# A two-stage bf16 kernel on one core: the order of a tie convolution, its copies and V's second half in the second and third bundle

## The chip, the core and the metric

The kernel runs on one core of one Trainium2 chip. The time is the device time of one execution in microseconds (us). A profile of one execution is at hand: what each engine did and when. The engines are TensorE (PE: matmuls, and PEld: weight loads), VectorE (DVE), ScalarE (ACT), GpSimd (POOL, which here issues loads) and SyncE (SP, which issues stores and transposing reads).

## The reference

First a causal convolution of 7 taps along the sequence, with one softmax-normalised set of taps for each of 8 heads of 24 columns. Its result goes into a channel mix: two mixtures of each row with the row before it, a projection to 1024 with relu and square, a projection back to 192, and a sigmoid gate.

```python
# x: 8 x 4160 x 192, weight: 8 x 7
out = einsum('hk,bskhg->bshg', softmax(weight), windows_of_7(x))     # -> x of the next part
x_prev = shift_by_one_row(x)
xk = mu_k * x + (1.0 - mu_k) * x_prev
xr = mu_r * x + (1.0 - mu_r) * x_prev
k = np.maximum(xk @ w_k, 0.0)          # 192 -> 1024
v = k * k @ w_v                        # 1024 -> 192
r = 1.0 / (1.0 + np.exp(-(xr @ w_r)))
return (r * v).astype(np.float32)
```

## The kernel before

The batch is worked in four pairs of sequences. A pair's 4160 rows are cut into steps of 512 rows (the first step of the first pair has 256). A step has eight **slots** (four for the step of 256). A slot is: the K matmuls of 128 of the 1024 hidden columns for both sequences into one PSUM tile of two banks (`k_mm`, L465, matmul L481), a relu out of PSUM on ScalarE (`k_relu`, L493), and a square on VectorE (`k_square`, L507). Four slots in a row make a **bundle**. So bundle 0 is step 0, bundles 1 and 2 are step 1, and so on. The text calls bundle 1 the second and bundle 2 the third; slot 2.1 is the first slot of the second bundle.

A **quad** is 256 rows of both sequences: the gate's matmuls and its sigmoid (`r`, L538 and L546), the V matmuls back to 192 columns (`v_rows`, L566, in two halves), the product with the gate (`v_out`, L582) and two stores (L590). The first quad is worked in the third bundle.

The convolution is a product with a banded matrix, over blocks of 120 rows. The rows are loaded by groups of blocks (`x_tile`, L100, with its memsets L106, L108 and L110; `load_x`, L112, with DMAs L120, L125 and L126 on GpSimd's queue); three buffers hold groups. The first three groups of the first pair (the **tie**) are convolved straight into the transposed layout that the mix needs: `conv_t` (L319), and `to_yT` (L329) copies the 128 x 480 fp32 result from PSUM to bf16. The second bundle does this for group 2, in three parts of 64 columns. Later groups go through `conv_mm` (L299) in units of two PSUM banks, and `conv_out` (L345), a ScalarE copy to a tile y. Group 3 is then transposed by TensorE (`tr`, L390, copies L399); from group 4 on, y goes to DRAM (`y_write`, L368) and comes back transposed (`y_read`, L376).

A unit of `conv_mm`, and a quad's V, is worked in two halves. In each half the upper and the lower 64 rows of the array write different banks; in the second half they change places. Between the halves stands an empty ScalarE instruction (`clobber_nop`, L307 and L574, called the **ticket** here): it waits for the first half, and the second half waits for it. It stands in ScalarE's order like any other instruction.

PSUM is one ring of four tiles of two banks (tag "k"), shared by slots, tie tiles, convolution units, gate, V and transposes. A tile that is asked for takes the buffer that is free next, and its first matmul waits until the last reader of that buffer is done.

The order is written by hand (`manual_schedule`): each engine runs its instructions in the order in which the functions `bundle_first`, `bundle_second` and `bundle_rest` call them. Work that has a due bundle stands in tables (`early`, `mix_a`, `mix_b`, `mix_c`, `late`, `rq`, `xt`, `vq`; L618), filled at L629 to L683 with `at`, and `run(table, b)` puts that bundle's entries at that point. `early` runs ahead of the bundle. In the second bundle `mix_a` runs after slot 2.4's matmuls and slot 2.1's square (L784, L785).

In `bundle_second` the three tie copies go to ScalarE, VectorE and ScalarE. In `bundle_rest` the third bundle (b == 2) has branches of its own: it transposes group 3 (L818 to L822), and its order after slot 3.3 is at L825 to L829 and L835 to L841.

Of the kernel before, what the change touches and what calls it, by code (L numbers as in the profile page):

```python
# [14 lines left out]
def kernel(  # L15
# [44 lines left out]
    for p in range(NPAIR):  # L60
# [5 lines left out]
        for L in sizes:  # L66
            ns = L * NF // STEP
# [210 lines left out]
    def conv_units(g):  # L278

        if groups[g][2] * 4 * G <= BANK:  # L280
            return [((0, 1), (6, 7)), ((2, 3), (4, 5))]
        return [((0,), (1,)), ((3,), (4,)), ((6,), (7,)), ((2,), (5,))]

    def conv_mm(g, c, half):

        nb = groups[g][2]
        if half == 0:
            if c == 0:
                ys[g] = two.tile([P, GB, 2 * D], BF16, tag="y", name="y")
            conv_ps[g, c] = ring.tile([P, 2, BANK], FP32, tag="k", name="ps_c")  # L290
        unit = conv_units(g)[c]
        last = len(unit[0]) - 1
        banks = conv_ps[g, c][:, :, 0 : nb * 2 * G * (last + 1)].rearrange("p i (n s c) -> p i n s c", n=nb, s=2)
        for k in range(last + 1):
            for i in range(2):
                q = slice(i * Q, (i + 1) * Q)
                bank = (i + half) % 2
                h = unit[bank][k]
                nc.tensor.matmul(  # L299
                    out=banks[:, bank, :, :, k * G : (k + 1) * G],  # L300
                    lhsT=toe[q, h, :],
                    rhs=xbs[g][q, :nb, :, h * G : (h + 1) * G],
                    start=half == 0 and k == 0,
                    stop=half == 1 and k == last,
                )
        if half == 0:
            nc.scalar.clobber_nop([nc.scalar.lower_ap(conv_ps[g, c])])  # L307
# [19 lines left out]
    def to_yT(g, c, o, b0, b1, copy):  # L327
        c0 = YC + (groups[g][1] + b0) * BLK
        copy(out=yTs[0][:, c, c0 : c0 + (b1 - b0) * BLK], in_=o[:, 0 : (b1 - b0) * BLK])  # L329
# [135 lines left out]
    def k_mm(n, cs=range(NC)):  # L465


        s, j = slots[n]
        L = steps[s][2]
        xk = xks[s]  # L470
        if cs[0] == 0 and n not in k_ps:
            k_ps[n] = ring.tile([P, 2, BANK], FP32, tag="k", name="ps_k")
        ps = k_ps[n]
        nf = STEP // L

        for c in cs:
            for f in range(nf):
                fs = slice((j * nf + f) * P, (j * nf + f + 1) * P)
                for i in range(2):
                    r = slice(i * Q, (i + 1) * Q)  # L480
                    nc.tensor.matmul(  # L481
                        out=ps[:, i, f * L : (f + 1) * L],
                        lhsT=wk[r, c, fs],
                        rhs=xk[r, c, :L],
                        start=c == 0 and f == 0,
                        stop=c == NC - 1 and f == nf - 1,
                    )

    def k_relu(n):
        ps = k_ps.pop(n)  # L490
        k_sb = four.tile([P, 2 * STEP], BF16, tag="k_sb", name="k_sb")
        k_sbs[n] = k_sb
        nc.scalar.activation(out=k_sb, in_=ps.rearrange("p a b -> p (a b)"), func=AF.Relu)  # L493

    def k_square(n):
        s, j = slots[n]
        L = steps[s][2]
        k_sb = k_sbs.pop(n)
        if j == 0:
            k2s[s] = three.tile([P, NF, 2 * STEP], BF16, tag="k2", name="k2")  # L500
        nf = STEP // L
        i = k_sb
        o = k2s[s][:, j, :]
        if nf > 1:
            i = k_sb.rearrange("p (b f t) -> p f b t", b=2, f=nf)
            o = k2s[s][:, j * nf : (j + 1) * nf, 0 : 2 * L].rearrange("p f (b t) -> p f b t", b=2)
        nc.vector.tensor_tensor(out=o, in0=i, in1=i, op=ALU.mult)  # L507
# [71 lines left out]
    def v_out(s, j):  # L579
        p, t0, L, _, _ = steps[s]  # L580
        o_sb = three.tile([P, 4, D], FP32, tag="o_sb", name="o_sb")
        nc.vector.tensor_tensor(  # L582
            out=o_sb.rearrange("p (b t) d -> p b (t d)", b=2),
            in0=v_ps.pop((s, j)),
            in1=r_sbs.pop((s, j)),
            op=ALU.mult,
        )
        for st in range(2):
            c = t0 + 2 * j * P
            nc.sync.dma_start(  # L590
                out=out[2 * p + st, c : c + 2 * P, :].rearrange("(m p) d -> p m d", p=P),
                in_=o_sb[:, 2 * st : 2 * st + 2, :],
            )
# [24 lines left out]
    early, rq, xt, mix_a, mix_b, mix_c, vq, late = ({} for _ in range(8))  # L618

    def at(table, b, fn, *a):  # L620
        table.setdefault(b, []).append((fn, a))

    def conv_half(unit, half):
        if unit is not None:
            conv_mm(*unit, half)
            if half == 1:
                conv_out(*unit, nc.scalar.copy)

    for g, (p, blk0, nb, fb, on_pe) in enumerate(groups):  # L629
        if g < 3:  # L630
            continue
        nx = len(conv_units(g))
        if p == 0:
            xs = {3: [1, 1], 4: [2, 2, 3, 3], 5: [4, 4, 5, 5]}[g]
        else:
            xs = range(fb - 10, fb - 10 + nx)
        for i, b in enumerate(xs):
            xt.setdefault(b, []).append((g, i))
        if not on_pe:
            at(late, xs[-1], y_write, g)  # L640

            at(mix_c if g == 4 else late, xs[-1] + (1 if g < 6 else 2), y_read, g)
        if g > 4:

            b = {5: 1, 6: 2, 7: 7}.get(g)
            b = first_bundle[first_step[p]] + (-15, -11, -7, -3)[(g - 6) % 4] if b is None else b
            at(mix_c if g == 7 else early, b, x_tile, g)
            at(mix_c if g == 7 else early, b, load_x, g)
    for s, (p, t0, L, n0, ns) in enumerate(steps):
        fb = first_bundle[s]  # L650
        if s == 0:
# [33 lines left out]
    def run(table, b):  # L685
        for fn, a in table.get(b, ()):
            fn(*a)
# [77 lines left out]
    def bundle_second(b, ns):  # L765

        act_, dve_ = nc.scalar.copy, nc.vector.tensor_copy
        g = 2
        k_mm(ns[0])
        k_relu(ns[0])  # L770
        k_mm(ns[1])
        tiles = [ring.tile([P, 2, BANK], FP32, tag="k", name="ps_t") for _ in range(2)]
        outs = [tiles[0][:, 0, :], tiles[1][:, 0, :], tiles[0][:, 1, :]]
        conv_t(g, 0, outs[0], range(4))
        to_yT(g, 0, outs[0], 0, 4, act_)
        k_relu(ns[1])
        conv_t(g, 1, outs[1], range(4))
        to_yT(g, 1, outs[1], 0, 4, dve_)
        k_mm(ns[2])
        k_relu(ns[2])  # L780
        conv_t(g, 2, outs[2], range(4))
        to_yT(g, 2, outs[2], 0, 4, act_)
        k_mm(ns[3])
        k_square(ns[0])  # L784
        run(mix_a, b)  # L785
        conv_half(xt[b][0], 0)
        k_relu(ns[3])
        conv_half(xt[b][0], 1)
        k_square(ns[1])
        run(mix_b, b)  # L790
        conv_half(xt[b][1], 0)
        conv_half(xt[b][1], 1)
        run(mix_c, b)
        run(late, b)

    def bundle_rest(b, ns):

        units = xt.get(b, []) + [None, None]
        quad = vq.get(b, [None])[0]
        for n in bundles[b - 1][2:]:  # L800
            k_square(n)
        run(mix_a, b)
        k_mm(ns[0])
        k_relu(ns[0])
        k_square(ns[0])
        if b > 2:
            run(mix_b, b)
            conv_half(units[0], 0)
        k_mm(ns[1])
        if b > 2:  # L810
            conv_half(units[0], 1)
        k_relu(ns[1])
        if b > 2:
            k_square(ns[1])
        run(rq, b)
        if quad:
            v_rows(*quad, 0)
        if b == 2:  # L818
            tr(3, 0)
            tr(3, 1)  # L820
            k_square(ns[1])
            run(mix_b, b)  # L822
        k_mm(ns[2])
        k_relu(ns[2])
        if b == 2:  # L825
            conv_half(units[0], 0)
            v_rows(*quad, 1)
            conv_half(units[0], 1)
            conv_half(units[1], 0)  # L829
        else:  # L830
            conv_half(units[1], 0)
            if quad:
                v_rows(*quad, 1)
                conv_half(units[1], 1)
        run(mix_c, b)  # L835
        k_mm(ns[3])
        if not quad or b == 2:
            conv_half(units[1], 1)
        k_relu(ns[3])
        if quad:  # L840
            v_out(*quad)  # L841
        run(late, b)

# [52 lines left out]
```

## Time and profile before

| | |
|---|---|
| Four runs | 418.88, 419.29, 417.96, 421.41 us; median 419.08 |
| Profiled execution | 418.88 us, of which the span of the engines' work is 417.0 |
| Granted TensorE clock | 1.00 of full speed |
| Busy in the span | PE 408.8 us (98%), DVE 377.7 (91%), ACT 348.1 (83%), POOL 51.9 (12%) |
| Stretch 17.39 to 33.35 us (second and third bundle, 15.96 us) | PE 14.96, DVE 13.63, ACT 15.17, POOL 7.26 |
| Stretch 60 to 400 us | PE 340.00 of 340.00, DVE 321.32, ACT 290.61 |

"Busy" of PE counts a matmul until its modelled end, so matmuls that overlap leave no gap, and short waits between them can hide in it. [...] the rows of the timeline show a slot's matmuls, six records of 512 columns, two at a time, taking 0.65 us of TensorE's order and ending 0.82 us after their start. A row of the timeline gives start, length, engine, line of the kernel, operation, output<-input, and, in brackets, how long the engine stood idle before and what released it; "issue" there is idle time for which the profile shows no releaser. The chain of waits follows the work that ended last back to the start.

### The profile page before, as it was taken

The page shows a single profiled execution, that of the slowest core. Times are in us where ns is not written, and L with a number is a line of the kernel's source. Part 1 is how long each engine was busy: PE and PEld are TensorE (multiplying, and loading weights), DVE is VectorE, ACT ScalarE, POOL GpSimd, SP SyncE. Part 2 cuts the span into 40 slices and gives each one's busy share as a digit, 9 for nine tenths or more (in the row PEclk, how much of TensorE's full clock was granted, in tenths as well). Part 3 has the DMA queues.
Part 4 walks back from the last instruction along what each step waited for, and adds up shares of the span by engine and source line. Part 5 has one row for each costly group of instructions (what it writes and reads, how often), then busy time and mean ns, then how long its engine had stood idle before and what let it go on. Part 6 is the DMA issues. An engine that isn't in the chain of part 4 may idle for free.

```text
span 417.0 us, 16360 instructions
## 1 busy us (share of the span) xinstructions
PE 408.8 (98%) x7135; PEld 317.6 (76%) x7136; DVE 377.7 (91%) x671; ACT 348.1 (83%) x409; POOL 51.9 (12%) x79
## 2 busy tenths in 40 slices
PE   6999999999999999999999999999999999999996
PEld 4667777777887777778778877877877787777886
DVE  5698789999999999999999999999999999999984
ACT  5899898898898889889888888988898798877781
POOL 7760003102030100202002010201100000000000
PEclk9999999999999999999999999999999999999999
DMA  9999779958599694959859694797936564411223
GB/s 150 162 191 185 189 182 188 235 141 167 136 184 239 144 207 118 134 171 186 187 128 210 172 176 126 148 235 129 185 103 154 139 164 124 118 58 60 77 79 115
DMA packets 134714, 64.59 MB, mean 155 GB/s; under 512 B 84190, under 2 KB 134642, under 8 KB 134642
## 3 DMA queue, kind: packets, MB, share of 16 engines
q1 hardware_dynamic: 95138, 48.32, 44.7%
q0 software_dynamic: 38704, 14.66, 31.1%
q8 instruction: 56, 0.92, 0.9%
q10 hardware_dynamic: 800, 0.57, 0.4%
q14 instruction: 16, 0.13, 0.1%
HBM read 29.89 MB, written 36.99 MB: 160 GB/s over the span
## 4 chain that ended last, share of the span: by engine, by line
PE 92%; ACT 4%; DMA 2%; issue 1%; DVE 0%; POOL 0%; ACTq 0%; POOLq 0%
PE ps_v L566 40%; PE ps_k L481 38%; PE ps_r L538 7%; PE ps_c L299 5%; ACT k_sb L493 3%; DMA xb<-in_x_dram 2%; PE ps_v L521 1%; PE ps_t L319 1%; ACT y L345 1%; ACT yT L329 0%; DVE o_sb L582 0%; POOL xb L126 0%; ACT r_sb L546 0%; DVE k L507 0%; DVE o_sb L602 0%
## 5 line engine op out<-in xcount | busy, mean ns | idle before, releaser
L493 ACT ACTIVATE k_sb<-ps_k 128x1024 bf16<-128x1024 f32 x260 | 261.5, 1040 | 53.7 <-PE ps_k L481 53.5
L481 PE MATMUL ps_k<-xk,wk 64*128 64x512 bf16 (+1 forms) x1632 | 201.6, 369 | 0.4 <-ACT y L345 0.2
L507 DVE TENSOR_TENSOR k<-k_sb 128x1024 bf16<-128x1024 bf16 x260 | 177.9, 687 | 15.4 <-ACT k_sb L493 8.3
L566 PE MATMUL ps_v<-wv,k 64*128 64x192 bf16 x4032 | 188.8, 243 | 0.7 <-ACT k_sb L493 0.4
L566 PEld LDWEIGHTS <-k 64*128 64x128 bf16 x4032 | 172.5, 94 | 13.8 <-issue 1.5
L481 PEld LDWEIGHTS <-wk 64*128 64x128 bf16 x1632 | 88.6, 95 | 51.6 <-issue 0.8
L582 DVE TENSOR_TENSOR o_sb<-ps_v,r_sb 128x768 f32<-128x768 f32 x64 | 61.2, 956 | 11.4 <-PE ps_v L566 4.5
L546 ACT ACTIVATE r_sb<-ps_r 128x768 bf16<-128x768 f32 x65 | 54.8, 846 | 0.0
L126 POOL DMA_DIRECT2D xb<-in_x_dram x34 | 30.8, 907 | 190.9 <-PE ps_c L299 92.3
L345 ACT CAST y<-ps_c 120x960 bf16<-120x960 f32 (+4 forms) x67 | 50.8, 788 | 2.4 <-PE ps_c L299 2.3
L538 PEld LDWEIGHTS <-xr 64*128 64x128 bf16 x780 | 36.1, 94 | 11.0 <-issue 0.4
L538 PE MATMUL ps_r<-wr,xr 64*128 64x192 bf16 x780 | 43.8, 243 | 0.0
L299 PE MATMUL ps_c<-xb,toe 64*128 64x480 bf16 (+2 forms) x240 | 39.2, 335 | 0.3
L455 DVE TENSOR_SCALAR xr<-d,mu 128x512 bf16<-128x512 bf16 (+1 forms) x102 | 35.8, 354 | 0.0
L424 DVE TENSOR_TENSOR d<-yT 128x1536 bf16<-128x1536 bf16 (+3 forms) x37 | 31.3, 847 | 2.4 <-ACT yT L329 2.3
L455 DVE TENSOR_SCALAR xk<-d,mu 128x512 bf16<-128x512 bf16 (+1 forms) x99 | 33.0, 360 | 0.1
L461 DVE TENSOR_TENSOR xr<-xr,yT 128x1536 bf16<-128x1536 bf16 (+1 forms) x33 | 31.0, 939 | 1.1
L461 DVE TENSOR_TENSOR xk<-xk,yT 128x1536 bf16<-128x1536 bf16 (+2 forms) x34 | 30.5, 896 | 0.1
L299 PEld LDWEIGHTS <-toe 64*128 64x128 bf16 x240 | 13.5, 94 | 12.2 <-issue 1.4
L408 POOL COPY y_tail<-yT 128x195 bf16<-128x195 bf16 x4 | 1.7, 424 | 68.6 <-DMA yT<-y_dram 68.6
L319 PEld LDWEIGHTS <-xb 128*32 128x32 bf16 (+3 forms) x264 | 5.3, 119 | 3.4 <-ACT xb L220 1.4
L319 PE MATMUL ps_t<-toe,xb 128*32 128x120 bf16 (+3 forms) x264 | 6.7, 272 | 1.1 <-DMA xb<-in_x_dram 0.6
(55 smaller groups left out, 58.0 us busy)
## 6 DMA issues: line engine op xcount, KB each, us to landing
out_dram<-o_sb SPq DMA_DIRECT2D x128, 192.0 KB, 2.6
y_dram<-y SPq DMA_DIRECT2D x10, 900.0 KB, 7.1
xb<-in_x_dram POOLq DMA_DIRECT2D x14, 480.0 KB, 7.8
xb<-in_x_dram POOLq DMA_DIRECT2D x6, 432.0 KB, 8.5
xb<-in_x_dram POOLq DMA_DIRECT2D x10, 192.0 KB, 5.1
y_dram<-y SPq DMA_DIRECT2D x3, 450.0 KB
y_dram<-y SPq DMA_DIRECT2D x1, 810.0 KB
wk<-in_moe_w_k_dram POOLq DMA_DIRECT2D x8, 96.0 KB, 5.1
```

The source lines that it names most:

```text
L299: nc.tensor.matmul(out=banks[:, bank, :, :, k * G : (k + 1) * G], lhsT=toe[q, h, :], rhs=xbs[g][q, :nb, :, h * G : (h + 1) * G], start=hal ...
L345: copy(out=bass.AP(tensor=y.tensor, offset=y.offset + d0, ap=[y.ap[0], [d1 - d0, 2], [2 * D, nb], [Q, 2], [1, n]],), in_=bass.AP(tensor=ps ...
L424: nc.vector.tensor_tensor(out=shaped(s, diffs[s][:, cs, :L]), in0=y_of(s, cs, 1), in1=y_of(s, cs, 0), op=ALU.subtract)
L455: nc.vector.tensor_scalar(out=t[:, c, :L], in0=diffs[s][:, c, :L], scalar1=mu[:, i, c : c + 1], scalar2=None, op0=ALU.mult)
L461: nc.vector.tensor_tensor(out=o, in0=o, in1=y_of(s, sl, 0), op=ALU.add)
L481: nc.tensor.matmul(out=ps[:, i, f * L : (f + 1) * L], lhsT=wk[r, c, fs], rhs=xk[r, c, :L], start=c == 0 and f == 0, stop=c == NC - 1 and f ...
L493: nc.scalar.activation(out=k_sb, in_=ps.rearrange("p a b -> p (a b)"), func=AF.Relu)
L507: nc.vector.tensor_tensor(out=o, in0=i, in1=i, op=ALU.mult)
L538: nc.tensor.matmul(out=ps[:, i, k * D : (k + 1) * D], lhsT=xr[q, c, ts], rhs=wr[q, c, :], start=c == 0, stop=c == NC - 1,)
L546: nc.scalar.activation(out=r_sbs[s, j], in_=ps[:, :, 0 : 2 * D], func=AF.Sigmoid)
L566: nc.tensor.matmul(out=v_ps[s, j][:, bank, k * D : (k + 1) * D], lhsT=k2s[s][q, f, t * P : (t + 1) * P], rhs=wv[q, f, :], start=half == 0 ...
L582: nc.vector.tensor_tensor(out=o_sb.rearrange("p (b t) d -> p b (t d)", b=2), in0=v_ps.pop((s, j)), in1=r_sbs.pop((s, j)), op=ALU.mult,)
```

## The change

Four edits, three of them in the second and third bundle's order:

- The x tile of group 5 and its load are called from `mix_a` of the second bundle, after slot 2.4's matmuls, and no longer from `early`, ahead of that bundle.
- The first of the three tie copies goes from ScalarE to VectorE, which then does two of three.
- In the third bundle, V's second half comes straight after slot 3.3, then `mix_c`, `v_out` and slot 3.4 with its relu; the two convolution units come after these, each with its two halves one after the other.
- The branches of the other bundles keep their order.

```diff
@@ filling the tables
-            at(mix_c if g == 7 else early, b, x_tile, g)
-            at(mix_c if g == 7 else early, b, load_x, g)
+            table = {5: mix_a, 7: mix_c}.get(g, early)
+            at(table, b, x_tile, g)
+            at(table, b, load_x, g)
@@ bundle_second
         conv_t(g, 0, outs[0], range(4))
-        to_yT(g, 0, outs[0], 0, 4, act_)
+        to_yT(g, 0, outs[0], 0, 4, dve_)
         k_relu(ns[1])
@@ bundle_rest
         k_mm(ns[2])
         k_relu(ns[2])
         if b == 2:
-            conv_half(units[0], 0)
             v_rows(*quad, 1)
-            conv_half(units[0], 1)
-            conv_half(units[1], 0)
+            run(mix_c, b)
+            v_out(*quad)
+            k_mm(ns[3])
+            k_relu(ns[3])
+            for unit in units[:2]:
+                conv_half(unit, 0)
+                conv_half(unit, 1)
         else:
             conv_half(units[1], 0)
             if quad:
                 v_rows(*quad, 1)
                 conv_half(units[1], 1)
-        run(mix_c, b)
-        k_mm(ns[3])
-        if not quad or b == 2:
-            conv_half(units[1], 1)
-        k_relu(ns[3])
-        if quad:
+            run(mix_c, b)
+            k_mm(ns[3])
+            if not quad:
+                conv_half(units[1], 1)
+            k_relu(ns[3])
+        if quad and b > 2:
             v_out(*quad)
         run(late, b)
```

In the built order TensorE, VectorE, ScalarE, GpSimd and SyncE have the same instructions as before, but for the one copy that changes its engine. From the fourth bundle on each engine's order is the same, and the four PSUM buffers follow the same turns under other names. In the second bundle the first convolution unit takes the buffer of the second tie tile, where before it took that of slot 2.3.

## The prediction

> **What bounds the kernel now.** I read the page's section on the chain of waits first, then the same chain cut to stretches, then each engine's timeline over the stretch that the edit touches.
>
> ```profile
> span 417.0 us, 16360 instructions
> PE 92%; ACT 4%; DMA 2%; issue 1%; DVE 0%; POOL 0%; ACTq 0%; POOLq 0%
> ...
> by line: PE ps_v L566 42.5%; PE ps_k L481 40.5%; PE ps_r L538 7.7%; PE ps_c L299 4.6%; ACT k_sb L493 1.4%; PE ps_v L521 1.4%; issue 0.4%; ACT y L345 0.3%; DVE o_sb L582 0.3%; DVE o_sb L602 0.1%; ACTq L345 0.0%
> ...
> by line: ACT k_sb L493 28.2%; PE ps_v L566 19.0%; PE ps_k L481 13.2%; PE ps_c L299 10.9%; issue 10.9%; ACT y L345 7.1%; ACT yT L329 6.4%; ACT r_sb L546 4.4%; DVE k L507 4.3%; ACTq L307 0.5%; ACTq L574 0.2%; ACTq L345 0.1%
> ```
>
> The second line is the whole chain, the third the chain from 33 us to the end, the fourth the chain from 17.3 to 33.6 us. After 33 us the chain is TensorE but for some 2.5%: whatever gets there earlier ends earlier by as much. Before 33 us nearly half of it is ScalarE. That stretch holds the second and third bundle, and all of the edit. ScalarE's timeline there (start, length, row, idle time before it):
>
> ```profile
> 18.28 0.58 ACT L329 CAST yT<-ps_t 128x480 bf16<-128x480 f32 x1
> 18.72 1.99 ACT L493 ACTIVATE k_sb<-ps_k 128x1024 bf16<-128x1024 f32 x2
> 20.54 0.62 ACT L329 CAST yT<-ps_t 128x480 bf16<-128x480 f32 x1
> 21.31 1.02 ACT L493 ACTIVATE k_sb<-ps_k 128x1024 bf16<-128x1024 f32 x1
> 22.23 1.88 ACT L345 CAST y<-ps_c 120x960 bf16<-120x960 f32 x3
> 23.96 1.99 ACT L493 ACTIVATE k_sb<-ps_k 128x1024 bf16<-128x1024 f32 x2
> 25.78 0.87 ACT L546 ACTIVATE r_sb<-ps_r 128x768 bf16<-128x768 f32 x1
> 26.47 1.50 ACT L399 COPY yT<-ps_t 128x720 bf16<-128x720 bf16 x2
> 27.76 1.14 ACT L493 ACTIVATE k_sb<-ps_k 128x1024 bf16<-128x1024 f32 x1
> 29.44 2.01 ACT L345 CAST y<-ps_c 120x960 bf16<-120x960 f32 x2 [0.55 <-PE ps_c L299]
> 31.35 1.95 ACT L493 ACTIVATE k_sb<-ps_k 128x1024 bf16<-128x1024 f32 x2
> ...
> 19.88 0.65 DVE L329 CAST yT<-ps_t 128x480 bf16<-128x480 f32 x1 [1.66 <-issue]
> 19.89 0.06 DVE L106 MEMSET xb<- 1x1 uint32 x1
> 20.45 0.68 DVE L507 TENSOR_TENSOR k<-k_sb 128x1024 bf16<-128x1024 bf16 x1
> ...
> 20.76 1.53 PE L299 MATMUL ps_c<-xb,toe 64*128 64x240 bf16 x16
> ...
> 31.51 0.82 PE L481 MATMUL ps_k<-xk,wk 64*128 64x512 bf16 x6 [0.17 <-ACT y L345]
> 33.35 1.50 PE L566 MATMUL ps_v<-wv,k 64*128 64x192 bf16 x32 [0.24 <-ACT k_sb L493]
> ```
>
> The reader is to see four things. ScalarE has no gap from 15.6 to 28.9 us except 0.15 before 21.31. VectorE stands 1.66 us before 19.88: its queue holds the one-element memset of the fifth x tile (L106), which waits for the third tie convolution, ahead of the tie copy. TensorE's first matmul of the fourth bundle's V (33.35) waits for a ScalarE relu (31.35, second of two: 32.27 to 33.30). That is the point to follow: V at 33.35.
>
> [...] the ticket (the empty ScalarE instruction at L307, which the second half of a convolution waits for) ended at 31.38 with the relu queued ahead of it starting only at 32.27. [...]
>
> **Second bundle, part by part.** Slots are called 2.1 to 2.4, 3.1 to 3.4, 4.1. Durations are from the rows above and from the single instructions that they merge; starts of successive ScalarE work lie 0.90 apart after a relu (17.38, 18.28), 0.84 after a 960-column copy (22.23, 23.07), 0.44 after a tie copy.
>
> The tie's first copy (18.28) leaves ScalarE, so relu 2.2 starts at 18.28, not 18.72. Relu 2.3 wants its matmuls, 18.46 + 0.83 = 19.29, so it starts at 19.32 (was 19.64). The third tie copy follows at 20.22 (was 20.54). Slot 2.4's matmuls wanted relu 2.2's buffer until 19.79; now it is free at 18.28 + 1.07 = 19.35, and TensorE comes to them at 19.66 from the third tie convolution, leaving them at 20.31 (3 pairs of 0.22). The first convolution half wanted relu 2.3's buffer (end 20.71, start 20.76); by the built order it now takes the second tie tile's, which a VectorE copy frees. So it runs at 20.31, done 20.67. Its ticket stands ahead of relu 2.4; before, that relu started 0.17 after the half was done (21.14, 21.31), so now 20.84. Gain 0.47. From there to 28.9 ScalarE ran without a gap, and its inputs (V's buffer, r, transposes) are released by ScalarE itself, so all of it shifts: relu 3.3 from 27.76 to 27.29.
>
> VectorE pays for the moved copy in its hole. It is free at 18.2, does two copies (18.2, 18.85, the second done at 19.5), squares slot 2.1 at 19.4 (was 20.45), then the memset after the third tie convolution (19.82), as before. The third tie convolution must wait for the first copy, done at 18.9, and starts at 19.22 anyway: 0.3 us of cover; a copy later than that costs its excess one for one. GpSimd's own memset (19.90) and the four DMAs behind it wait for the same convolution as before, and the DMA that also needs VectorE's memset starts at 21.16, so the load moves nowhere: at nothing. The next x load sits behind a memset that moves earlier with VectorE by about 0.9; its data is first read after 50 us: at nothing.
>
> **Third bundle.** Nothing is added or taken away, only order. Before, ScalarE had relu 3.3, two convolution copies, relu 3.4, relu 4.1; it waited 0.55 for the first copy, because V's second half (1.32: 16 pairs of 0.083) ran ahead of the convolution's. Now relu 3.3, relu 3.4, copies, relu 4.1. TensorE: slot 3.3 at 26.24 (the sigmoid before it 0.47 earlier), V's half 26.89 to 28.21, slot 3.4 to 28.86, done 29.04. Relu 3.4 at 29.07; ScalarE was free at 27.29 + 0.92 = 28.21, so a new idle of 0.86 replaces the old 0.55 and 0.09. Convolution halves now follow each other with the ticket between: in the second bundle the same pair measured first half 21.44, second half 21.91, so 0.27 beyond its own 0.20. So: first unit 28.86, second half 29.33, done 29.71; copy at 29.07 + 0.92 = 29.99 (waits for ScalarE, not TensorE: 0.28 cover). Second unit 29.53, second half 30.00, done 30.38; copy at 30.83 (0.45 cover). Slot 4.1's matmuls 30.20 to 30.85, done 31.02; relu 4.1 at 30.83 + 0.84 = 31.67 (0.65 cover), against 32.27. Queued behind the tickets are just these copies and relu 4.1. The earlier V copy (L582) frees its PSUM buffer at about 29.5, before slot 4.1 asks (30.20). V of the fourth bundle: 31.67 + 1.03 + 0.05 = 32.75, against 33.35.
>
> Sum: 0.47 + 0.13 = 0.60 us gained. After that the order and (renamed) buffers are those of before, so the shift stays. Profiled execution 418.88 (span 417.0 and 1.88 around it): 418.3. The median of the four runs is 419.08, so 418.5.
>
> The one cost that the trace doesn't show is how early the three close tickets pass. Best, each passes as its half is done (used above). Worst, each passes only when the ScalarE work ahead of it has ended: priced as a rival below, 0.5 us on the other side. I take the first, because of the ticket at 31.38.
>
> **Rivals.**
> 1. *The reorder hands the gain back.* The 0.86 idle grows, or the 0.3 us cover of the tie copy fails; gain 0 to 0.2. For: the new idle is longer than the old. Against: covers of 0.28 to 0.65 downstream. 418.9 to 419.1.
> 2. *TensorE's waits go altogether.* From 17.39 to 33.35 (15.96 us) TensorE's own work adds up to about 12.8 (slots 2.3 to 4.2, eight of 0.65: 5.2; V 2.64; convolution halves 0.8 and 1.2; tie 1.2; transposes 0.75; r twice 0.5), so 3.2 is waiting. If two thirds go, 2.1: 417.0. For: VectorE comes 1 us earlier. Against: ScalarE's work in that stretch, 15.17 busy of 15.96, falls only by the one copy.
> 3. *Slower: tickets wait for ScalarE to finish.* Place: the convolution halves of the third bundle. Relu 3.4 ends at 30.10; second half 30.15, done 30.53, copy 30.55 to 31.51; next second half 31.55, done 31.93, copy 31.95, relu 4.1 at 32.79, V at 33.87: 0.5 later than before, 419.6. It decides from where V starts after 33.35. Against: the ticket at 31.38 named above.
>
> [...]
>
> **How the numbers follow.** Forecast (gain 0.2 to 1.2) 0.60; rival 1 0.15; rival 2 0.14; rival 3 0.11. About 0.5%, 2.1 us, is what a measurement of this kernel can tell from no change, so the forecast and rival 1 are no change; rival 2 is faster nearly whole, and a little of the forecast's upper edge and of the spread of runs (417.96 to 421.41) with it: 0.15. Of rival 3 perhaps half is over 2.1 us, if more tickets meet it in later bundles: 0.06. The range, 416.8 to 420.0, leaves out the far half of rivals 2 and 3; the forecast's own is 417.6 to 419.4.
>
> **What would show it.** ScalarE's second row of L329 gone near 18.28; VectorE's hole of 1.66 gone, its two L329 rows near 18.2 and 18.85; relu 2.4 near 20.84; relu 3.3 near 27.29; a ScalarE idle of 0.86 before relu 3.4 near 29.07; V of the fourth bundle near 32.75 with the chain after it on TensorE as before. Wrong if V starts after 33.2 or before 32.0, or if the chain after 33 us shows more than 2.5% off TensorE.

## The result, and the profile after

| | Before | After |
|---|---|---|
| Median, us | 418.73 (55 runs, 417.66 to 421.77) | 417.42 (34 runs, 416.65 to 419.65) |
| Ratio after to before | | 0.9966, 95% interval 0.9957 to 0.9976 |
| Span of the profiled execution, us | 417.0 | 415.6 |

The change takes 1.0 to 1.8 us off, more than the 0.6 forecast. Of the runs after, the three with a mean granted clock of 0.996 took 419.20 to 419.65 us, all others at most 418.19. The two lines of the page after that answer to those of before:

```profile
span 415.6 us, 16363 instructions
...
PE 92%; ACT 2%; issue 1%; DVE 0%; ACTq 0%
```

TensorE's share of the chain is as before; ScalarE's is 2% in place of 4%, and the 2% of DMA is no longer named. ScalarE's timeline after:

```profile
18.54 1.02 ACT L493 ACTIVATE k_sb<-ps_k 128x1024 bf16<-128x1024 f32 x1 [0.15 <-PE ps_k L481]
19.46 0.55 ACT L329 CAST yT<-ps_t 128x480 bf16<-128x480 f32 x1
20.16 1.02 ACT L493 ACTIVATE k_sb<-ps_k 128x1024 bf16<-128x1024 f32 x1
...
26.76 1.04 ACT L493 ACTIVATE k_sb<-ps_k 128x1024 bf16<-128x1024 f32 x1
28.39 1.02 ACT L493 ACTIVATE k_sb<-ps_k 128x1024 bf16<-128x1024 f32 x1 [0.59 <-PE ps_k L481]
29.31 1.82 ACT L345 CAST y<-ps_c 120x960 bf16<-120x960 f32 x2
31.00 1.06 ACT L493 ACTIVATE k_sb<-ps_k 128x1024 bf16<-128x1024 f32 x1
```

VectorE's timeline after, and then TensorE's:

```profile
17.38 1.22 DVE L329 CAST yT<-ps_t 128x480 bf16<-128x480 f32 x2
18.52 0.68 DVE L507 TENSOR_TENSOR k<-k_sb 128x1024 bf16<-128x1024 bf16 x1
...
19.14 0.06 DVE L106 MEMSET xb<- 1x1 uint32 x1
```

```profile
25.56 0.82 PE L481 MATMUL ps_k<-xk,wk 64*128 64x512 bf16 x6
26.21 1.50 PE L566 MATMUL ps_v<-wv,k 64*128 64x192 bf16 x32
27.52 0.83 PE L481 MATMUL ps_k<-xk,wk 64*128 64x512 bf16 x6
28.34 1.52 PE L299 MATMUL ps_c<-xb,toe 64*128 64x480 bf16 x8
...
32.11 1.50 PE L566 MATMUL ps_v<-wv,k 64*128 64x192 bf16 x32
```

The edits are all to be seen. Slot 3.3 starts at 25.56. One tie copy is left on ScalarE (19.46); VectorE makes the other two back to back at 17.38, and the one-element memset comes after them (19.14) with no hole. V's second half (26.21) and slot 3.4 (27.52) run ahead of the convolution (28.34). V of the fourth bundle starts at 32.11, 1.24 before the 33.35 of before. From there nothing changes: a relu that starts at 401.83 before starts at 400.59 after, 1.24 again, and the spans differ by 1.4. The same holds for every kernel that was profiled here: the time of the profiled execution less the start of this V is 385.3 to 385.5 us in all twelve profiles. So the question is what happened ahead of 33 us.

The two profiles don't start alike, though: the tie convolution begins at 17.39 before and 16.72 after, and the code ahead of it is the same. The landings of the loads at the start differ from one execution to the next: TensorE stood 0.65 us for an x load ahead of 9.24 in the profile before, and in the one after not there, but 1.06 us for wk ahead of 14.67 (more landings in the tables below). A difference of single profiles is therefore no gain; distances inside one profile, and times over many runs, have to settle it.

### The profile page after: what moved, and what is told of

Its sections match the earlier page's. It is cut to its first block, busy times and chain, and to the rows that moved or that the text cites. A ratio compares the mean times of both kernels' runs of the same rounds, so it can differ in the third digit from the quotient of the medians.

```text
span 415.6 us, 16363 instructions
## 1 busy us (share of the span) xinstructions
PE 407.3 (98%) x7135; PEld 317.0 (76%) x7136; DVE 378.2 (91%) x672; ACT 347.7 (84%) x408; POOL 51.9 (12%) x79
## 4 chain that ended last, share of the span: by engine, by line
PE 92%; ACT 2%; issue 1%; DVE 0%; ACTq 0%
PE ps_v L566 40%; PE ps_k L481 38%; PE ps_r L538 7%; PE ps_c L299 5%; ACT k_sb L493 2%; PE ps_v L521 1%; ACT y L345 0%; DVE o_sb L582 0%; PE ps_t L390 0%; DVE o_sb L602 0%; ACTq L307 0%; ACTq L345 0%
## 5 line engine op out<-in xcount | busy, mean ns | idle before, releaser
L126 POOL DMA_DIRECT2D xb<-in_x_dram x34 | 30.7, 906 | 190.8 <-PE ps_c L299 92.3
```

## Experiments

All times are medians beside runs of the kernel before on the same chip. Three theories stand against each other: the order of the third bundle gains by itself; the copy that leaves ScalarE gains; or, after the second profile of before, a wait that the forecast did not name is what the change removes.

**The two kernels once more.** No edit.

> The kernel before, a second profile of it. Chance theory: the 0.7 us by which the changed kernel's profile came earlier to the second bundle (first tie convolution at 16.72 against 17.39) is the loads of the start, which differ from run to run; then this profile may enter anywhere from 16.5 to 17.8, and the stretch from the tie convolution's start to V of the fourth bundle is again 16.0 (15.8 to 16.2). Entry theory: the stretch itself depends on how the start went (ScalarE or TensorE behind); then the stretch comes out different by more than 0.3. Time ratio 1.000.

> The changed kernel, a second profile of it. Chance theory: stretch from the tie convolution to V 15.4 again, entry anywhere from 16.5 to 17.8. Entry theory: stretch anywhere from 14.7 to 15.4, shorter where TensorE enters late. Time ratio 0.9966 again.

Before: 418.74 us, 1.0003 [0.9990, 1.0017], span 416.6. After: 417.30 us, 0.9966 [0.9954, 0.9978], span 416.0. The gain is real. The stretch from the tie to V was 16.46 us before (16.0 expected) and 15.76 after (15.4 expected), so the stretch isn't of a fixed length that merely starts earlier or later. The new profile of before is the more telling one. Its waits between 22 and 34 us (for whom, total, times, longest), and then its chain of waits from 25 to 34 us (start, length, what):

```profile
ACT y L345 <- PE ps_c L299: 1.3, 1, 1.3
...
PE ps_c L299 <- DMA xb<-in_x_dram: 0.7, 1, 0.7
```

```profile
16.33 10.70 DMA xb<-in_x_dram
27.03 0.14 issue
27.16 0.38 PE ps_c L299 x2
27.54 1.32 PE ps_v L566 x32
...
32.97 0.04 issue
33.01 1.00 PE ps_v L566 x20
```

TensorE's timeline of the same profile, where the first row is slot 3.3:

```profile
25.60 0.82 PE L481 MATMUL ps_k<-xk,wk 64*128 64x512 bf16 x6 [0.16 <-ACT r_sb L546]
27.16 0.38 PE L299 MATMUL ps_c<-xb,toe 64*128 64x480 bf16 x2 [0.74 <-DMA xb<-in_x_dram]
27.37 1.50 PE L566 MATMUL ps_v<-wv,k 64*128 64x192 bf16 x32
```

The third bundle's convolution reads the x tile of group 4. The last half of that tile is loaded by a DMA (L126) issued at 16.33, and lands at 27.03; TensorE was done with slot 3.3 and stood 0.74 us for it. In the old order, V's half, slot 3.4 and everything else of the bundle is queued behind that first convolution half. ScalarE's idle of 1.3 us before its convolution copy holds the same wait, one step on (in the old order without the wait, below, the same idle is 0.29 to 0.39).

The first profile of before had this wait too, but only 0.15 us of it:

```profile
26.71 0.82 PE L481 MATMUL ps_k<-xk,wk 64*128 64x512 bf16 x6 [0.16 <-ACT r_sb L546]
27.51 0.38 PE L299 MATMUL ps_c<-xb,toe 64*128 64x480 bf16 x2
```

There the load landed at 27.37, and TensorE could have gone on from slot 3.3 at about 27.36 (26.71 + 0.65). The convolution started at 27.51, some 0.14 after the landing, as in every profile where the load came last. Since a matmul's record lasts until its modelled end (26.71 + 0.82 = 27.53), no row shows a gap.

**One part of the change at a time.** The second bundle's edits alone:

```diff
+            table = {5: mix_a, 7: mix_c}.get(g, early)
...
-        to_yT(g, 0, outs[0], 0, 4, act_)
+        to_yT(g, 0, outs[0], 0, 4, dve_)
```

> The second bundle's edits alone (copy to VectorE, x tile of group 5 from mix_a); the third bundle in its old order. If the prediction's split is right (0.47 of 0.60 here), the time falls by about 1.0 of the 1.3 us measured for the whole: ratio 0.9975. If the third bundle carries the gain, by 0.3 or less: 0.9993.

And the third bundle's order alone, in two sets of runs (the start of the edit; the rest is the third part of the change):

```diff
         if b == 2:
-            conv_half(units[0], 0)
             v_rows(*quad, 1)
-            conv_half(units[0], 1)
-            conv_half(units[1], 0)
+            run(mix_c, b)
+            v_out(*quad)
+            k_mm(ns[3])
+            k_relu(ns[3])
+            for unit in units[:2]:
+                conv_half(unit, 0)
+                conv_half(unit, 1)
```

> The third bundle's new order alone; the second as before. If the prediction's split is right (0.13 of 0.60), the time falls by about 0.1 to 0.3 us: ratio 0.9995. If the third bundle carries the gain, by 1.0: 0.9976.

> The third bundle's new order alone, a second time, for its time (the first profile of it had a TensorE clock of 0.50 from 16 to 18 us) . Ratio 0.9966 again if the second bundle's edits add nothing beside it; 0.9975 to 0.998 if they add the 0.4 to 0.5 us of the prediction. V of the fourth bundle near 32.3.

The second bundle's edits alone: 418.77 us, 1.0007 [0.9996, 1.0017]: nothing that can be told. The third bundle's order alone: 417.55 us, 0.9966 [0.9948, 0.9984], and again 417.44 us, 0.9973 [0.9960, 0.9985]: the whole gain, as far as runs can tell. (V of the fourth bundle was expected near 32.3 in the second of these; it came at 32.88, in an execution of 418.25 us.) TensorE's timeline of the kernel with the second bundle's edits alone:

```profile
25.93 0.82 PE L481 MATMUL ps_k<-xk,wk 64*128 64x512 bf16 x6
27.30 0.38 PE L299 MATMUL ps_c<-xb,toe 64*128 64x480 bf16 x2 [0.55 <-DMA xb<-in_x_dram]
...
33.14 1.08 PE L566 MATMUL ps_v<-wv,k 64*128 64x192 bf16 x22 [0.24 <-ACT k_sb L493]
```

TensorE waits 0.55 us for the same load. The landings, taken from the trace's DMA records, set beside what follows:

| Profile | Tie starts | Load of group 4 landed | Its convolution starts | V of the fourth bundle | V less landing |
|---|---|---|---|---|---|
| Before (first) | 17.39 | 27.37 | 27.51 | 33.35 | 5.98 |
| Before (again) | 16.55 | 27.03 | 27.16 | 33.01 | 5.98 |
| Second bundle's edits alone | 16.79 | 27.16 | 27.30 | 33.14 | 5.98 |
| After (first) | 16.72 | 28.21 | 28.34 | 32.11 | 3.90 |
| After (again) | 16.70 | 28.52 | 28.66 | 32.46 | 3.94 |
| Third bundle's order alone (first) | 18.57 | 27.40 | 30.24 | 34.17 | 6.77 |
| Third bundle's order alone (again) | 16.71 | 27.66 | 28.95 | 32.88 | 5.22 |

In the old order V of the fourth bundle starts 5.98 us after the landing, to the hundredth, in three profiles whose tie starts differ by 0.84. The landing decides; 0.2 us won in the second bundle is waited for at the convolution. The new order lets V's half and slot 3.4 go first: in the profiles of after the load landed 0.84 to 1.49 us later than in those of before, and V still came earlier. (The first profile with the third bundle's order alone ran with a lowered clock before its tie; the last section shows it.)

The copy without the moved x tile wasn't tried: in VectorE's order the memset for that tile, which held the engine for 1.66 us in the first profile of before, would stand ahead of the first copy. It waits for the third tie convolution, which would wait for that copy, a circle (worked out from the order, not run). Nor was the moved tile tried without the copy; the two were measured together only.

**The wait taken away in the old order.** The first two convolution units of group 4 read wk, which has long landed (by 14.3 us in these runs), with the same strides:

```diff
+    def rhs_of(g, c, q, h):
+        if g == 4 and c < 2:
+            return wk[q].rearrange("p a b -> p (a b)")[:, 0:2880].rearrange("p (n s w) -> p n s w", n=10, s=2)[:, :, :, h * 8 : h * 8 + G]
+        return xbs[g][q, : groups[g][2], :, h * G : (h + 1) * G]
...
-                    rhs=xbs[g][q, :nb, :, h * G : (h + 1) * G],
+                    rhs=rhs_of(g, c, q, h),
```

> The kernel before in its old order, but the third bundle's two convolution units (group 4, units 0 and 1) multiply parts of the K weights, with the same strides, in place of x of group 4: their results are another computation, and they no longer need the load of group 4. Load theory (the third bundle's convolution waited for the second half of that load, which landed at 27.03 to 27.37 us in the profiles): the first convolution matmul starts when slot 3.3's are done, near 26.2, and the time falls by 0.8 to 1.3 us, ratio 0.997 to 0.998. Order theory (the gain of the new order comes from ScalarE and ticket order, not from the load): ratio 0.9995 to 1.0005.

> The same exchange of data, and the second bundle's two edits on top (copy on VectorE, x tile of group 5 from mix_a). If those edits are worth the 0.47 us of the prediction once no load pins the third bundle: 0.4 to 0.5 us faster than the run with the exchange alone. If V's weights, which landed at 22.0 to 23.4 us, pin V's first half instead: 0 to 0.2 us faster.

In the order of before: 417.57 us, 0.9978 [0.9970, 0.9987]. With the second bundle's edits as well: 417.25 us, 0.9970 [0.9960, 0.9980]. TensorE's timeline of the first of the two (line numbers are 5 higher in this kernel):

```profile
25.19 0.82 PE L486 MATMUL ps_k<-xk,wk 64*128 64x512 bf16 x6 [0.16 <-ACT r_sb L551]
25.83 0.38 PE L304 MATMUL ps_c<-wk,toe 64*128 64x480 bf16 x2
26.03 1.50 PE L571 MATMUL ps_v<-wv,k 64*128 64x192 bf16 x32
...
31.68 1.50 PE L571 MATMUL ps_v<-wv,k 64*128 64x192 bf16 x32 [0.25 <-ACT k_sb L498]
```

The convolution now follows slot 3.3 after 0.64 (25.19, 25.83), while the load lands at 26.50. Its own row is as long as before (0.38), so the other data didn't make it cheaper. Without any new order, most of the gain is there. That shows the wait to be worth about a microsecond. It doesn't yet tell whether the new order has a worth of its own. The second bundle's edits on top came out 0.32 us faster, between the two expectations (0.4 to 0.5, or 0 to 0.2), and the intervals overlap.

**The wait taken away in both orders.** If the order gained by itself, it would add to the wait that is gone. The edit is the one above, put on the kernel with the third bundle's order alone, and beside it the old order is run once more.

> The third bundle's new order, and the first two convolution units of group 4 multiply wk data in place of x (other computation, same strides), so that neither order waits for group 4's load. Alone against the kernel before, the new order gave 0.9966 and 0.9973, the missing load wait in the old order 0.9978. Theory (both remove the same wait, the order adds 0.1 to 0.3 us of its own): together 0.996 to 0.9975, 417.0 to 417.7 us, and the distance from relu 3.3 to relu 4.1 about 4.2 to 4.3 us. Rival (the order gains about 1.2 us of its own, whatever the load does): the two add up, 0.994 to 0.9955, 416.2 to 416.9 us, with that distance near 3.4.

> The old order with the first two convolution units of group 4 multiplying wk data in place of x (other computation), once more beside the run above. Theory and rival alike: 0.997 to 0.9985, 417.5 to 418.2 us. Theory: the run above is at most 0.5 us below it; rival: 1 us or more below it.

| Third bundle's order | Waits for group 4's load | Reads wk, no wait |
|---|---|---|
| Old | 1 | 0.9978 [0.9970, 0.9987]; 0.9968 [0.9957, 0.9980] |
| New | 0.9966 [0.9948, 0.9984]; 0.9973 [0.9960, 0.9985] | 0.9976 [0.9966, 0.9987] |

They don't add up: the new order on top of the missing wait gave 417.47 us, the old order beside it 417.38 (a little below the 417.5 expected). ScalarE's and TensorE's timelines in the new order without the wait:

```profile
26.32 1.13 ACT L498 ACTIVATE k_sb<-ps_k 128x1024 bf16<-128x1024 f32 x1
28.09 1.02 ACT L498 ACTIVATE k_sb<-ps_k 128x1024 bf16<-128x1024 f32 x1 [0.64 <-PE ps_k L486]
...
30.70 1.05 ACT L498 ACTIVATE k_sb<-ps_k 128x1024 bf16<-128x1024 f32 x1
...
25.26 0.82 PE L486 MATMUL ps_k<-xk,wk 64*128 64x512 bf16 x6 [0.16 <-ACT r_sb L551]
...
31.81 1.50 PE L571 MATMUL ps_v<-wv,k 64*128 64x192 bf16 x32 [0.22 <-ACT k_sb L498]
```

From relu 3.3 to relu 4.1 it takes 4.38 us (26.32, 30.70), a little over the 4.2 to 4.3 expected and far from the rival's 3.4. This distance is a rough measure, since relu 3.3 itself can start late and make up for it in the idle behind it. The distance from slot 3.3 to V of the fourth bundle, both on TensorE, is sharper:

| Third bundle's order | Profiles | Slot 3.3 to V, us |
|---|---|---|
| Old, waits for the load | before (first, again); second bundle's edits alone | 6.64, 7.41, 7.21 |
| Old, no wait | the three that read wk | 6.49 in each |
| New, waits for the load or not | after (both); third bundle's order alone (both); the one that reads wk | 6.54 to 6.55 in each |

So the wait cost 0.15, 0.92 and 0.72 us in the three profiles of the old order (6.64, 7.41 and 7.21 less 6.49). The new order takes all of it off the path: 6.55 even in the two profiles of after, where the load held the convolution for 0.13 to 0.17 us. For itself it gains nothing. Free of the wait, it is some 0.05 us longer than the old order.

**Slot 3.4 ahead of V's second half.** The 0.59 us of ScalarE's idle before relu 3.4 is still there in the changed kernel. If it costs, slot 3.4 should go first:

```diff
         if b == 2:
+            k_mm(ns[3])
+            k_relu(ns[3])
             v_rows(*quad, 1)
             run(mix_c, b)
             v_out(*quad)
-            k_mm(ns[3])
-            k_relu(ns[3])
```

> The changed kernel with slot 3.4 ahead of V's second half in the third bundle, to take away ScalarE's idle time before relu 3.4 (0.59 us measured). If ScalarE's order decides the third bundle: relu 3.4 follows relu 3.3 at 0.92, V of the fourth bundle 0.3 to 0.6 us earlier, ratio 0.9955. If TensorE or the load of group 4 (landed at 28.2 to 28.5 us in the two profiles of the changed kernel) decides by then: 0.9964 to 0.9968, as the changed kernel.

417.15 us, 0.9964 [0.9952, 0.9976]: not to be told from the changed kernel. TensorE's timeline, and ScalarE's:

```profile
25.01 1.47 PE L481 MATMUL ps_k<-xk,wk 64*128 64x512 bf16 x12 [0.16 <-ACT r_sb L546]
26.30 1.50 PE L566 MATMUL ps_v<-wv,k 64*128 64x192 bf16 x32
28.18 1.52 PE L299 MATMUL ps_c<-xb,toe 64*128 64x480 bf16 x8 [0.39 <-ACT k_sb L493]
...
31.87 1.50 PE L566 MATMUL ps_v<-wv,k 64*128 64x192 bf16 x32
```

```profile
26.07 2.05 ACT L493 ACTIVATE k_sb<-ps_k 128x1024 bf16<-128x1024 f32 x2
29.07 1.82 ACT L345 CAST y<-ps_c 120x960 bf16<-120x960 f32 x2 [0.95 <-PE ps_c L299]
```

The idle before relu 3.4 is gone (two relus in a row at 26.07), and comes back as 0.95 before the copy. The row of 28.18 names ScalarE's relu as what ended TensorE's wait. That relu, 3.4, ended at 28.12; group 4's load landed at 28.05, and 28.18 is again 0.13 after it. The two came within 0.1 us of each other, so this profile can't part them, but without the relu the load would still have held the convolution about there. From slot 3.3 (25.01 here) to V (31.87) it takes 6.86 us, 0.31 more than in the changed kernel: this order loses to the wait what the other doesn't. V came 3.68 us after the convolution here, and 3.76 and 3.80 after it in the profiles of after, so there, too, a load that landed some 0.1 us later would have begun to count (an estimate from these three).

## Why the prediction was right, and where its working was not

**The landmarks after.** The forecast set them for a tie that starts at 17.39. In the first profile of after it started at 16.72, 0.67 earlier:

| | Forecast less 0.67 | Measured |
|---|---|---|
| Relu 2.4 | 20.17 | 20.16 |
| Relu 3.3 | 26.62 | 26.76 |
| Relu 3.4, ScalarE idle ahead of it | 28.40, 0.86 | 28.39, 0.59 |
| V of the fourth bundle | 32.08 | 32.11 |

The third bundle's new order was worked out well: slot 3.3 to V is 6.51 us in the forecast (26.24, 32.75), and 6.54 to 6.55 in all five profiles that have this order. That the whole stretch met within 0.03 us is in part luck. From the tie to slot 3.3 the forecast had 8.85, the first profile of after 8.84, the second 9.22, and there V came at 32.46, 0.4 later. (The idle of 0.86 was reckoned from where the next ScalarE work could start, 0.92 after relu 3.3; reckoned so, the measured one is 0.71.) VectorE's hole went, as forecast.

**The term that failed: the third bundle's 0.13.** The working took the old order's path through the third bundle from the first profile (slot 3.3 to V 6.64) as one of ScalarE and TensorE alone, set the new order's 6.51 against it, and called the difference of 0.13 the worth of the order. But 0.15 of the 6.64 was the wait for the load; ScalarE's idle of 0.55, put down to V's second half, held it too. The load didn't come as much earlier as the engines did: in the two other profiles of the old order slot 3.3 started 1.10 and 0.78 us earlier (25.60 and 25.93 against 26.71), the load landed 0.34 and 0.21 earlier, and TensorE's path lost 0.92 and 0.72. The first profile, with its late tie, was the one that hid it. Measured, the order by itself costs some 0.05 us, and the load wait 0.15 to 0.92 us in the profiles and 0.5 to 1.8 us in the two sets of runs that took it away in the old order ((1 - 0.9987) and (1 - 0.9957) of 418.7).

**The second bundle's 0.47.** Locally it was 0.21 in the first profile of after and 0.34 in the second (relu 2.1 to relu 3.1: 6.58 before, in both profiles; 6.37 and 6.24 after). The other profiles with these edits have 6.37, 6.37, and 6.84 where the tie waited 0.55 for a load of its own. The forecast took TensorE's place from the first profile, where the tie starts 0.01 after relu 2.1. In the first profile of after it starts 0.27 after (16.45, 16.72), and relu 2.3 comes 1.18 after relu 2.2 (17.36, 18.54), where 1.04 was forecast; in the second, with the tie 0.23 ahead of relu 2.1, it comes 1.06 after. Of this gain no run shows anything in the time: alone it ends at the load (1.0007), and on top of the new order (0.9966 against 0.9966 and 0.9973) or of the missing wait (0.9970 against 0.9978 and 0.9968) the intervals overlap. Up to 0.3 us may be there. In both profiles of after, the V weights land late (23.05 and 23.35) and V's first half starts 0.14 later, but this took nothing back: slot 3.3 starts 2.74 us after relu 3.1 in both, as before (2.75 and 2.74). Something else may have: in five of the twelve profiles TensorE stood 0.24 to 0.88 us in the middle of the gate's matmuls, with no releaser shown, and in three of them slot 3.3 came 0.30 to 0.57 us later for it. Its cause stays open; it falls on kernels with and without these edits.

"At nothing" for group 5's moved load fits: its four DMAs come after group 4's in GpSimd's queue, and nothing reads them in this stretch. With the second bundle's edits alone group 4 landed at 27.16, between the 27.03 and 27.37 of before.

**The rivals.** The first, that the reorder hands the gain back, was wrong of the time and near the truth of the order itself, which gains nothing; but not for the reason given: the new idle was no longer than forecast, and the covers downstream held (the convolution copy started at 29.31, when relu 3.4 let go of ScalarE, not when TensorE was done). The second needed 2.1 us of waits to go; 1.0 to 1.8 went. It was nearest in kind: a wait of TensorE went, though only 0.15 of the 3.2 us that it counted in that profile was this one, and the working set only ScalarE's busy time against it. The third, tickets that wait for ScalarE to finish, is false here too: the single instructions show the second unit's second half at 29.49, while the first unit's copy, queued ahead of its ticket, ran on ScalarE from 29.31 to 30.26.

The time came out inside the range because the range, 416.8 to 420.0, was wide, the missed wait was about 1 us and the second bundle's 0.47 went largely unpaid. The gain of the medians, 1.3 us (418.73 less 417.42), is more than twice the forecast's 0.60, and 417.42 lies just below the forecast's own 417.6 to 419.4. So the outcome was right in good part by luck.

**The step left out.** The working never set the landing of a load beside its first reader in this stretch, group 5's and later ones apart. The record of the issue doesn't show the landing: in the second profile of before GpSimd's record at 16.33 is over in 0.96 us, and the data lands 10.7 us after it began. What the DMA engines move meanwhile, all queues together, by stretches of 2 us:

| Stretch, us | 18 to 20 | 20 to 22 | 22 to 24 | 24 to 26 | 26 to 28 |
|---|---|---|---|---|---|
| Before (again), GB/s | 191 | 194 | 192 | 190 | 192 |
| After (first), GB/s | 188 | 194 | 192 | 190 | 193 |
| After (again), GB/s | 154 | 184 | 192 | 191 | 194 |

From 22 us on the rates are alike, while the landing differs: 27.03, 28.21 and 28.52. The latest came where less was moved before 22 us. What else sets the landing, and whether the change makes it later, was not settled: with the third bundle's order alone it was 27.40 and 27.66.

## What to carry to other kernels

When a stretch early in a kernel reads data for the first time, set every load's landing beside its first reader before working out the engines' chain: a gain ahead of a load that lands last was worth nothing here (1.0007), and moving the work that doesn't need the load ahead of its reader took the whole wait off the path (0.15 to 0.92 us in the profiles). One profile can hide such a wait when the engine happens to come as late as the load does, as the first one here did (0.15 us); a distance that stays the same to the hundredth over several profiles, as 5.98 us here, gives it away. To tell a better order from an avoided wait, take the wait away in both orders and see whether the gains add; and compare, on one engine, the distance from the last work ahead of the wait to the point where the path is the same again. Here this told 0.05 us apart, where the times of the runs left several tenths open.

## What the runs showed of the hardware

The first profiled execution of the third bundle's order alone took 419.68 us, with a mean granted clock of 0.996. TensorE had waited 1.91 us for the last parts of wk. The windows of that profile (length; busy time and records of TensorE, its weight loads, VectorE, ScalarE, GpSimd; granted clock; DMA; GB/s), then TensorE's row after the wait, and the same row in the second profile of this kernel:

```profile
14.00:16.00 2.00, 1.41 (x13) 0.91 (x15) 1.68 (x3) 0.09 (x1) 1.42 (x3) 0.71 1.53 180
16.00:18.00 2.00, 2.00 (x13) 1.37 (x11) 0.58 (x1) 1.38 (x2) 1.65 (x2) 0.50 1.58 187
18.00:20.00 2.00, 2.00 (x75) 1.06 (x70) 0.11 (x1) 1.44 (x3) 0.00 (x0) 0.93 1.58 185
...
14.59 4.05 PE L481 MATMUL ps_k<-xk,wk 64*128 64x256 bf16 x24 [1.91 <-DMA wk<-in_moe_w_k_dram]
...
14.45 2.32 PE L481 MATMUL ps_k<-xk,wk 64*128 64x256 bf16 x24 [2.02 <-DMA wk<-in_moe_w_k_dram]
```

The clock fell to 0.50 at 14.85, when TensorE was already at work again, and stayed there for 3.41 us (the trace's clock record; the windows have 0.71, 0.50 and 0.93). The same 24 matmuls took 4.05 us in place of 2.32, and the tie began at 18.57 in place of 16.71. The second profile had waited a little longer, 2.02 us, and its row of 2.32 shows no such drop (mean granted clock 0.999), so the length of the wait alone doesn't decide it. What brought the drop about was not tested. It came behind a late load in this execution, and cost about as much again as the wait itself (1.73 us on the 24 matmuls, 4.05 less 2.32, against 1.91).
